# Queries and keys loaded in runs of 2 KB: two tokens of one head per transpose, even and odd tokens evicted apart, a ring of six tiles

## The chip, the core and the metric

The kernel runs on one core of a Trainium2 chip. The metric is device time in microseconds, from the start of the program to its end. A core has TensorE (PE in the profile, with its weight loads as PEld), VectorE (DVE), ScalarE (ACT), GpSimd (POOL) and SyncE (SP), which here only issues DMAs. PE's clock is granted by the chip: 1.00 in the profile is 2.4 GHz, 0.50 is 1.2 GHz.

## What is computed

Attention over short bands, and then a layer of eight experts of which each token takes one (batch 8, 8 heads, 576 tokens, head size 64):

```python
scores = scale * np.matmul(q, k.transpose(0, 1, 3, 2))
rel = pos[:, None] - pos[None, :]
mask_plain = (rel >= 0) & (rel < window)                                      # heads 0 to 3, window 32
mask_dil = (rel >= 0) & (rel < window * dilation) & (rel % dilation == 0)     # heads 4 to 7, dilation 4
...
attn = attn / (np.sum(attn, axis=-1, keepdims=True) + 1e-09)
attn_out = np.matmul(attn, v)
x = attn_out.transpose(0, 2, 1, 3).reshape(B * S, H * D)                      # 4608 tokens x 512
logits = x @ w_gate + modality_bias[modality_id]
e_idx = np.argmax(logits, axis=1)
...
h = np.maximum(x[mask] @ w1[e], 0.0)                                          # 512 -> 1024 -> 512
out[mask] = gate_w[mask, None] * (h @ w2[e])
```

All of it is fp32.

## The kernel before

**Heads and units.** The heads of a batch come in two kinds (`kd`): plain (0) and dilated (1), four heads each. Dilated heads have their tokens sorted by their rest modulo 4, so that their mask too becomes a band of 32. A tile is 64 queries against 96 keys: its own 64 and the 32 ahead of them. A unit is two tiles of four heads, 128 rows; a batch has nine units, the fifth with one tile of either kind. 72 units in all, in a list `order`.

**Turns.** One loop over t (I call a step of it a turn, and t modulo 9 the turn of the batch) issues in turn t: the scores of unit t, the exponential of t - 1, the attention of t - 3 (probabilities times V), the logits of t - 5, the normalization of t - 3, the transposes of the probabilities of t - 2, the store of t - 4 (a transpose of its x, and a DMA on POOL's queue), and two pieces of work for the next batch. PE, DVE, ACT and SP run their instructions in the order written; POOL's order is set by a scheduler, but for the calls made through the object `pool`, which keep theirs.

**Queries and keys.** `load_one` (L112) loads one kind of q or k of one batch, [96 partitions, 6 tokens, 4 heads, 64] in 4 DMAs, one for each head; partition p holds tokens 6p to 6p + 5. The tiles are named `st`, and there are four of them in a ring. `qk_chunks` (L283) makes six pieces of one kind of one batch. A piece takes two of the six token places: four transposes of [96, 2 heads x 64] into a PSUM tile of 384 columns (keys from the pool `ps_t`, three tiles named pt; queries from `psum['o']`, three tiles named po), and ACT copies it out, in one instruction of 384 elements (plain) or two of 192 (dilated), with tokens at their places in `qT` and `kT`. The copy of queries also scales by 1/8. The pieces of the next batch's plain heads come in turns 4 to 6, those of its dilated heads in turn 8 and turns 0 and 1 of the next batch. The loads are issued at the end of turns 1 and 2 (dilated) and 6 and 7 (plain), and wait until PE has read the tile that is four back.

**V.** `load_v` fetches V of one kind into one of three buffers `vw`, in rows 32 to 95 of a tile: one DMA for the plain heads (turn 3), twelve for the dilated ones (six at the end of turn 8, six in turn 0). Rows 0 to 31 of a tile are the last 32 of the tile before. `shift_v` copies them within SBUF in a single DMA (vw<-vw in the profile, L137), in turn 8 for the next batch's plain heads and in turn 3 for the dilated ones:

```python
nc.sync.dma_start(out=t[0:WIN, :, 1:NTILE].rearrange("p h i d -> p h (i d)"),
                  in_=t[TQ:KW, :, 0:NTILE - 1].rearrange("p h i d -> p h (i d)"))
```

The dilated heads are first used by the scores of turn 4, and their V by the attention in turn 7. All these DMAs stand in SP's one queue, in the order of the program, and a DMA whose wait isn't over holds what is behind it.

**The other work.** When the logits of a batch are done, `gating` chooses the experts and scatters the tokens' numbers into a table. After batch 4 three slots of 256 tokens are set up early: the generator `background` gathers the rows of slot 0, splits them (`prepare_x`) and issues six pieces of weight loads, two turns of the generator apart, once t has reached 63. The generators go on twice in a turn. In turn 70 the expert stage (`slots`) begins to be mixed in. It runs on through the 19 slots.

## Time and profile before

| | us |
|---|---|
| median of 3 runs (732.46 to 734.91) | 734.7 |
| the profiled execution | 731.71 |
| its span, first to last instruction | 729.8 |
| PE busy in the span | 659.7 (90%) |
| DVE busy | 500.3 (69%) |
| ACT busy | 411.9 (56%) |
| POOL busy | 292.1 (40%) |

The span is cut into 40 slices of 18.2 us. The first 16 are attention, the rest the experts. In the row PEclk a digit is the granted clock of a slice in tenths (9 is 0.9 or more). The chain of work that ended last names only the final 11 us, so the attention stage is read from the waits and from the order of time.

### The profile page before, as it was taken

The page shows a single profiled execution, that of the slowest core. Times are in us where ns is not written, and L with a number is a line of the kernel's source. Part 1 is how long each engine was busy: PE and PEld are TensorE (multiplying, and loading weights), DVE is VectorE, ACT ScalarE, POOL GpSimd, SP SyncE. Part 2 cuts the span into 40 slices and gives each one's busy share as a digit, 9 for nine tenths or more (in the row PEclk, how much of TensorE's full clock was granted, in tenths as well). Part 3 has the DMA queues.
Part 4 walks back from the last instruction along what each step waited for, and adds up shares of the span by engine and source line. Part 5 has one row for each costly group of instructions (what it writes and reads, how often), then busy time and mean ns, then how long its engine had stood idle before and what let it go on. Part 6 is the DMA issues. An engine that isn't in the chain of part 4 may idle for free. (4 is left out here: it accounts for less than half of the span.)

```text
span 729.8 us, 17822 instructions
## 1 busy us (share of the span) xinstructions
PE 659.7 (90%) x6286; PEld 581.2 (80%) x6286; DVE 500.3 (69%) x1212; ACT 411.9 (56%) x900; POOL 292.1 (40%) x396
## 2 busy tenths in 40 slices
PE   5798789799687888989999999999999999999991
PEld 3686678687576767879999999998999999999980
DVE  1478579588586786786777666777666776667660
ACT  3476467477454544545656565566565666565550
POOL 7334557467465764564333133232132322220110
PEclk7599799799887868999999999999999999999996
DMA  9797796969967692423434583332323326831730
GB/s 161 134 220 174 161 197 154 211 141 188 185 140 165 183 239 76 101 73 111 123 95 124 169 223 87 102 116 74 102 73 102 116 75 164 239 92 54 189 93 12
DMA packets 165536, 99.20 MB, mean 136 GB/s; under 512 B 124400, under 2 KB 143346, under 8 KB 165444
## 3 DMA queue, kind: packets, MB, share of 16 engines
q1 hardware_dynamic: 148916, 68.15, 42.5%
q0 software_dynamic: 11120, 28.64, 12.8%
q10 hardware_dynamic: 5408, 1.24, 1.1%
q8 instruction: 51, 0.84, 0.5%
q14 instruction: 41, 0.34, 0.2%
HBM read 127.52 MB, written 29.39 MB: 215 GB/s over the span
## 5 line engine op out<-in xcount | busy, mean ns | idle before, releaser
L855 PE MATMUL pt<-xh,w1l 128*128 128x256 f32 (+1 forms) x608 | 172.5, 284 | 3.2 <-DVE w1l L804 3.2
L855 PE MATMUL pt<-xl,w1h 128*128 128x256 f32 (+1 forms) x608 | 172.3, 283 | 0.0
L855 PE MATMUL pt<-xh,w1h 128*128 128x256 f32 (+1 forms) x608 | 172.2, 283 | 0.1
L861 ACT ACTIVATE hh<-pt 128x256 fp32r<-128x256 f32 (+1 forms) x152 | 57.6, 379 | 165.7 <-PE pt L855 165.7
L278 POOL DMA_INDIRECT xr<-x_dram,idt x74 | 84.6, 1144 | 122.9 <-DMA x_slot<-xr 83.9
L804 DVE TENSOR_TENSOR w2l<-w2q,w2h 128x512 fp32r<-128x512 f32 x152 | 104.9, 690 | 41.3 <-ACT w2h L803 33.1
L855 PEld LDWEIGHTS pt<-xh,w1h 128*128 128x128 f32 x608 | 116.7, 192 | 7.0 <-ACT w1h L803 0.4
L855 PEld LDWEIGHTS pt<-xl,w1h 128*128 128x128 f32 x608 | 116.8, 192 | 5.7
L855 PEld LDWEIGHTS pt<-xh,w1l 128*128 128x128 f32 x608 | 116.6, 192 | 4.0 <-DVE w1l L804 4.0
L835 PE MATMUL py<-w2h,hh 128*128 128x512 f32 x296 | 117.6, 397 | 0.0
L835 PE MATMUL py<-w2h,hl 128*128 128x512 f32 x296 | 116.8, 395 | 0.0
L835 PE MATMUL py<-w2l,hh 128*128 128x512 f32 x296 | 116.0, 392 | 0.0
L862 DVE SCALAR_TENSOR_TENSOR hl<-pt,hh 128x256 fp32r<-128x256 f32 (+1 forms) x152 | 63.4, 417 | 75.7 <-ACT hh L861 75.6
L278 POOL DMA_INDIRECT out_dram<-ys,idt x37 | 39.2, 1059 | 177.7 <-ACT ys L838 115.0
L804 DVE TENSOR_TENSOR w1l<-w1q,w1h 128x512 fp32r<-128x512 f32 x152 | 103.9, 684 | 1.8 <-ACT w1h L803 1.7
L803 ACT CAST w1h<-w1q 128x512 fp32r<-128x512 f32 x152 | 94.5, 622 | 2.3 <-DMA w1q<-in_moe_w_dram 2.3
L803 ACT CAST w2h<-w2q 128x512 fp32r<-128x512 f32 x152 | 93.1, 612 | 0.1
L359 ACT COPY pT<-pt 96x512 f32<-96x512 f32 x72 | 41.8, 581 | 89.3 <-PE pt L356 88.3
L365 PE MATMUL po<-vw,pT 96*64 96x65 f32 x1152 | 58.3, 247 | 28.3 <-DMA vw<-vw 19.5
L278 POOL TENSOR_TENSOR sm<-sm,nmx 128x384 f32<-128x384 f32 x72 | 59.8, 831 | 55.6 <-DVE den L372 32.3
L365 PEld LDWEIGHTS po<-vw,pT 96*64 96x64 f32 x1152 | 46.7, 155 | 40.3 <-issue 13.9
L835 PEld LDWEIGHTS py<-w2l,hh 128*128 128x128 f32 x296 | 55.7, 188 | 13.2
(159 smaller groups left out, 1114.2 us busy)
## 6 DMA issues: line engine op xcount, KB each, us to landing
w2q<-in_moe_w_dram SPq DMA_DIRECT2D x76, 512.0 KB
w1q<-in_moe_w_dram SPq DMA_DIRECT2D x152, 256.0 KB
st<-in_k_dram SPq DMA_DIRECT2D x64, 144.0 KB
x_slot<-xr SPq DMA_DIRECT2D x18, 512.0 KB
xg<-x_slot SPq DMA_DIRECT2D x72, 128.0 KB
x_dram<-x_sb POOLq DMA_DIRECT2D x32, 256.0 KB
st<-in_q_dram SPq DMA_DIRECT2D x56, 144.0 KB
vw<-in_v_dram SPq DMA_DIRECT2D x8, 576.0 KB
```

The source lines that it names most:

```text
L278: ins = tc.keep_in_program_order(getattr(nc.gpsimd, name)(*args, **kw))
L359: nc.scalar.copy(out=self.pT, in_=src)
L365: nc.tensor.matmul(out=pov[u * TQ:(u + 1) * TQ, h, :], lhsT=self.pT[:, h, u * TQ:(u + 1) * TQ], rhs=self.vts[kd][:, h, i, :], start=True, ...
L803: nc.scalar.copy(out=hi, in_=raw)
L804: nc.vector.tensor_tensor(out=lo, in0=raw, in1=hi.bitcast(F32), op=ALU.subtract)
L835: nc.tensor.matmul(out=py[u], lhsT=ht[:, us], rhs=wt, start=(f + n == 0), stop=(f + n == FC + 1))
L855: nc.tensor.matmul(out=ph, lhsT=wt[:, c, :], rhs=xt[:, c, 0:cols], start=(c + i == 0), stop=(c + i == KC + 1))
L861: nc.scalar.activation(out=hh, in_=ph, func=AF.Relu)
L862: nc.vector.scalar_tensor_tensor(out=hl, in0=ph, scalar=0.0, in1=hh.bitcast(F32), op0=ALU.max, op1=ALU.subtract)
```

## The change

Loading: a DMA now brings two heads of q or k, [72 partitions, 2 heads, 8 tokens, 64], so each run is 8 tokens of one head, 2 KB. A batch has eight such loads (numbered n; k and q alternate), 64 in all, and the tiles form a ring of six. Load n is issued at the end of the turn whose pieces read load n - 6.

Pieces: one piece is one head of one load. Four transposes of [72, 2 tokens x 64] put an even token's 64 features in PSUM partitions 0 to 63 and the odd one's in 64 to 127; the outputs stand at a step of 4 words (plain) or 2 words (dilated), so that the tile's 288 columns are in order. ACT then copies the two halves apart, 64 partitions x 288 elements each. A batch has 16 pieces, two per turn in turns 4 to 8 and 0 to 2 (three per turn at the very start).

Beside that, a product in `gating` is issued through `pool`, and slot 0's `prepare_x` stands three turns or so later, between the weight loads.

```diff
-PQ = 96
+PQ = 72
 SI = S // PQ
+QKBUFS = 6
...
-        t = ald.tile([PQ, SI, 4, D], F32, name="st")
-        for h in range(4):
-            queue.dma_start(out=t[:, :, h], in_=src[b, 4 * kd + h].rearrange("(p s) d -> p s d", s=SI))
-        return t
...
+        b, i = divmod(n, 8)
+        h = 4 * (i // 4) + 2 * (i // 2 % 2)
+        t = ald.tile([PQ, 2, SI, D], F32, name="st")
+        queue.dma_start(out=t.rearrange("p a s d -> p a (s d)"),
+                        in_=(q if i % 2 else k)[b, h:h + 2].rearrange("a (p s) d -> p a (s d)", s=SI))
+        staged[n] = t
...
-            for g in range(2):
-                for i in range(2):
-                    nc.tensor.transpose(out=pt[:, PQ * (2 * g + i):PQ * (2 * g + i + 1)],
-                                        in_=src[:, 2 * n + i, 2 * g:2 * g + 2].rearrange("p a d -> p (a d)"), identity=ident[:PQ, :PQ])
...
+            half = pt[:, 0:S // 2]
+            for j in range(SI // 2):
+                if kd == 0:
+                    to = half.rearrange("c (p j) -> c p j", j=SI // 2)[:, :, j]
+                else:
+
+                    to = half.rearrange("c (k p t) -> c k p t", k=2, t=2)[:, j % 2, :, j // 2]
+                nc.tensor.transpose(out=to, in_=src[:, a, 2 * j:2 * j + 2].rearrange("p i d -> p (i d)"), identity=ident[:PQ, :PQ])
+            flat = (qT[kd] if is_q else kT[kd][:, :, WIN:])[D * a:D * (a + 1), g]
+            for i in range(2):
+                inp = half[D * i:D * (i + 1)]
+                if kd == 0:
+                    dst = flat.rearrange("c (x i) -> c x i", i=2)[:, :, i]
+                else:
+                    dst = flat.rearrange("c (k i x) -> c k i x", k=2, i=2)[:, :, i]
+                    inp = inp.rearrange("c (k x) -> c k x", k=2)
...
-        (nc.vector if b == B - 1 else nc.gpsimd).tensor_tensor(out=t0, in0=t0, in1=ewt, op=ALU.mult)
+        (nc.vector if b == B - 1 else pool).tensor_tensor(out=t0, in0=t0, in1=ewt, op=ALU.mult)
...
-            for _ in range(6):
+            for _ in range(3):
                 load_more(0, 1)
                 yield
+                yield
+            steps = prepare_x(0, ids_of[0])
+            for i in range(6):
+                if i % 2 == 0:
+                    load_more(0, 1)
+                next(steps, None)
                 yield
...
+    for n in range(QKBUFS, 8 * B):
+        b, i = divmod(n - QKBUFS, 8)
+        at = (-1 if i < 4 else 1 + (2 * (i - 4) + 1) // 3) if b == 0 else 9 * (b - 1) + 4 + i
+        load_at.setdefault(at, []).append(n)
...
-            if m == 1:
-                state['k', 1] = load_one(b + 1, 1, k)
-            elif m == 2:
-                state['qk', b + 1, 1] = load_one(b + 1, 1, q), state['k', 1]
-            elif m == 6 and b + 2 < B:
-                state['k', 0] = load_one(b + 2, 0, k)
-            elif m == 7 and b + 2 < B:
-                state['qk', b + 2, 0] = load_one(b + 2, 0, q), state['k', 0]
...
+        for n in load_at.get(t, ()):
+            load_qk(n)
```

How it stands on the engines, at three places. First SP's queue around the copy of V's rows for the dilated heads of batch 1 (turn 3; vw0 is its buffer, the last row the V load of the next batch's plain heads). Before:

```order
L131 DMA vw0_104<-in_v_dram 64x4x64 x2
L116 DMA st_982<-in_k_dram 96x6x64 x4
L116 DMA st_1035<-in_q_dram 96x6x64 x4
L137 DMA vw0_104<-vw0_104 32x4x520
L127 DMA vw1_105<-in_v_dram 64x36x64
```

Now:

```order
L132 DMA vw0_104<-in_v_dram 64x4x64 x2
L118 DMA st_960<-in_q_dram 72x2x512
L118 DMA st_1026<-in_k_dram 72x2x512
L118 DMA st_1090<-in_q_dram 72x2x512
L138 DMA vw0_104<-vw0_104 32x4x520
L128 DMA vw1_105<-in_v_dram 64x36x64
```

Between the last V loads and the copy stood eight load DMAs, issued at the end of turns 1 and 2; now three stand there, one for each of turns 0, 1 and 2.

Second ACT, in a turn with pieces of plain heads (pe: the exponential, pT: the copy of the transposed probabilities, uxh: the high part of x). Before:

```order
L359 COPY pT<-pt 96x512
L391 CAST uxh<-pt 128x256
L311 COPY kT_101<-pt 128x2x2x96
L309 ACTIVATE qT_100<-po 128x2x2x96
L351 ACTIVATE pe<-sm 128x384
```

Now, from a turn's keys to the next turn's queries:

```order
L316 COPY kT_101<-pt 64x288 x4
L356 ACTIVATE pe<-sm 128x384
L364 COPY pT<-pt 96x512
L396 CAST uxh<-pt 128x256
L314 ACTIVATE qT_100<-po 64x288 x4
```

Two copies of 384 elements on 128 partitions have become four of 288 elements on 64, and a turn is all keys or all queries.

Third PE, in the same kind of turn, with the numbers of the PSUM tiles (pt from the ring of three; pe and x_sb are the sources of the transposes of probabilities and of x). Before:

```order
L356 MATMUL pt_890<-ident_128,pe_720 96x128 x4
L387 MATMUL pt_897<-ident_128,x_sb_805 128x128 x2
L294 MATMUL pt_904<-ident_128,st_392 128x96 x4
L294 MATMUL po_911<-ident_128,st_450 128x96 x4
L340 MATMUL pss_918<-kT0_101,qT0_100 64x96 x8
```

Now, a turn of keys:

```order
L361 MATMUL pt_848<-ident_120,pe_685 96x128 x4
L392 MATMUL pt_855<-ident_120,x_sb_778 128x128 x2
L304 MATMUL pt_864<-ident_120,st_473 128x72 x4
L304 MATMUL pt_871<-ident_120,st_473 128x72 x4
L345 MATMUL pss_893<-kT0_101,qT0_100 64x96 x8
```

A turn took three tiles pt and one po for these; a turn of keys now takes four tiles pt, and the fourth is the first one's buffer again.

## Rows read from the trace of the kernel before

**Rows 1.** The page: span, granted clock in 40 slices, DMA packets.

```profile
span 729.8 us, 17822 instructions
PEclk7599799799887868999999999999999999999996
DMA packets 165536, 99.20 MB, mean 136 GB/s; under 512 B 124400, under 2 KB 143346, under 8 KB 165444
```

**Rows 2.** Windows: length, PE, PEld, DVE, ACT, POOL busy (instructions), clock, DMA share, GB/s.

```profile
340.00:729.00 389.00, 373.56 (x2391) 338.15 (x2389) 264.07 (x464) 225.31 (x466) 101.80 (x93) 0.99 0.41 116
```

**Rows 3.** Timeline of PE, 45 to 79 us: start, duration, instructions [idle before, releaser].

```profile
45.80 0.60 PE L356 MATMUL pt<-ident,pe 128*96 128x128 f32 x4
...
48.05 0.60 PE L356 MATMUL pt<-ident,pe 128*96 128x128 f32 x4
...
48.71 0.49 PE L294 MATMUL pt<-ident,st 96*128 96x96 f32 x4
49.04 0.49 PE L294 MATMUL po<-ident,st 96*128 96x96 f32 x4
...
50.82 0.63 PE L356 MATMUL pt<-ident,pe 128*96 128x128 f32 x4
...
68.42 0.60 PE L356 MATMUL pt<-ident,pe 128*96 128x128 f32 x4
...
76.80 1.10 PE L365 MATMUL po<-vw,pT 96*64 96x65 f32 x14 [5.23 <-DMA vw<-vw]
...
78.23 1.05 PE L356 MATMUL pt<-ident,pe 128*96 128x128 f32 x4
```

**Rows 4.** Waits of PE, 0 to 300 us: total us, times, longest.

```profile
PE po L365 <- DMA vw<-vw: 19.5, 7, 5.9
...
PE pt L294 <- DMA st<-in_k_dram: 4.4, 2, 2.7
PE po L294 <- DMA st<-in_q_dram: 4.0, 2, 2.1
```

**Rows 5.** Windows of 5 us after the first long wait.

```profile
75.00:80.00 5.00, 3.20 (x32) 2.75 (x36) 0.95 (x4) 0.62 (x2) 0.00 (x0) 0.50 0.96 213
80.00:85.00 5.00, 5.00 (x90) 4.34 (x82) 3.87 (x13) 2.72 (x9) 3.25 (x5) 0.75 0.90 185
```

**Rows 6.** Timeline of PE: the two other long waits.

```profile
137.41 1.10 PE L365 MATMUL po<-vw,pT 96*64 96x65 f32 x14 [5.01 <-DMA vw<-vw]
...
198.26 1.13 PE L365 MATMUL po<-vw,pT 96*64 96x65 f32 x14 [5.91 <-DMA vw<-vw]
```

**Rows 7.** Timeline of SP's queue, 53 to 70 us.

```profile
53.80 9.67 SPq L131 DMA_DIRECT2D vw<-in_v_dram  x12
63.99 2.65 SPq L116 DMA_DIRECT2D st<-in_k_dram  x4
66.75 2.63 SPq L116 DMA_DIRECT2D st<-in_q_dram  x4
69.42 0.71 SPq L137 DMA_DIRECT2D vw<-vw  x1
```

**Rows 8.** Timeline of ACT, one turn with plain pieces.

```profile
66.34 0.58 ACT L359 COPY pT<-pt 96x512 f32<-96x512 f32 x1 [0.72 <-PE pt L356]
66.82 0.37 ACT L391 CAST uxh<-pt 128x256 fp32r<-128x256 f32 x1
67.09 0.88 ACT L311 COPY kT<-pt 128x384 f32<-128x384 f32 x1
67.73 0.94 ACT L309 ACTIVATE qT<-po 128x384 f32<-128x384 f32 x1
68.43 0.56 ACT L351 ACTIVATE pe<-sm 128x384 f32<-128x384 f32 x1
```

**Rows 9.** Timeline of DVE: slot 0's first transpose.

```profile
252.01 0.71 DVE L787 STREAM_TRANSPOSE xt<-xg 128x512 f32<-128x512 f32 x1 [1.57 <-DMA xg<-x_slot]
```

**Rows 10.** Timeline of ACT: a dilated pair, two instructions merged.

```profile
25.43 0.67 ACT L311 COPY kT<-pt 128x192 f32<-128x192 f32 x2
```

More of the change, by code (lines that the diff above doesn't have):

```diff
@@ L138, in shift_v @@
                           in_=t[TQ:KW, :, 0:NTILE - 1].rearrange("p h i d -> p h (i d)"))
-    state = {('qk', 0, 0): load_qk(0, 0, nc.scalar)}
+    state = {}
+    for n in range(4):
+        load_qk(n, nc.scalar if n % 2 else nc.sync)
     state['v', 0, 0] = load_v(0, 0)
-    state['qk', 0, 1] = load_qk(0, 1, nc.scalar)
+    for n in range(4, QKBUFS):
+        load_qk(n, nc.scalar if n % 2 else nc.sync)
     ident = cpool.tile([P, P], F32, name="ident")
@@ L308, in chunk @@
+            for i in range(2):
[5 more added lines that the diff above has]
+                    inp = inp.rearrange("c (k x) -> c k x", k=2)
                 if is_q:
-                    nc.scalar.mul(dst, src, 1.0 / 8.0)
+                    nc.scalar.mul(dst, inp, 1.0 / 8.0)
                 else:
-                    nc.scalar.copy(out=dst, in_=src)
@@ L312, in qk_chunks @@
-        return [(lambda n=n, is_q=is_q: chunk(n, is_q)) for n in range(SI // 2) for is_q in (False, True)]
+                    nc.scalar.copy(out=dst, in_=inp)
+        return [(lambda n=n, a=a: chunk(n, a)) for n in range(8 * b + 4 * kd, 8 * b + 4 * kd + 4) for a in range(2)]
     def mask_of(kd, i):
@@ L739, in background @@
                 yield
-            for _ in range(4):
-                yield
-            yield from prepare_x(0, ids_of[0])
             while state['t'] < (B - 1) * 9:
                 yield
-            for _ in range(6):
+            for _ in range(3):
                 load_more(0, 1)
                 yield
+                yield
[4 more added lines that the diff above has]
+                next(steps, None)
                 yield
@@ L917 @@
     man.enter_context(tc.manual_schedule(engines=MANUAL))
-    for ch in qk_chunks(0, *state['qk', 0, 0]):
+    for ch in qk_chunks(0, 0):
         ch()
-    state['qk', 1, 0] = load_qk(1, 0)
     shift_v(0, 1)
+    load_at = {}
+    for n in range(QKBUFS, 8 * B):
+        b, i = divmod(n - QKBUFS, 8)
+        at = (-1 if i < 4 else 1 + (2 * (i - 4) + 1) // 3) if b == 0 else 9 * (b - 1) + 4 + i
+        load_at.setdefault(at, []).append(n)
+    for n in load_at[-1]:
+        load_qk(n)
     credit = 0.0
@@ L949 @@
         if t == 1:
-            pieces = qk_chunks(1, *state['qk', 0, 1])
+            pieces = qk_chunks(0, 1)
         if t < NU:
@@ L956 @@
                 if m == 4:
-                    pieces = qk_chunks(0, *state['qk', b + 1, 0])
+                    pieces = qk_chunks(b + 1, 0)
                 elif m == 8:
-                    pieces = qk_chunks(1, *state['qk', b + 1, 1])
+                    pieces = qk_chunks(b + 1, 1)
                     shift_v(b + 1, 0)
@@ L992 @@
             units[t - 4].keep(pool)
-        for i in range(2):
-            step()
+        at_once = 3 if t < 4 else 2
+        for i in range(at_once):
+            if i < 2:
+                step()
             if i < len(pieces):
                 pieces[i]()
-        pieces = pieces[2:]
-        if t < NU and b + 1 < B:
-            if m == 1:
-                state['k', 1] = load_one(b + 1, 1, k)
-            elif m == 2:
-                state['qk', b + 1, 1] = load_one(b + 1, 1, q), state['k', 1]
-            elif m == 6 and b + 2 < B:
-                state['k', 0] = load_one(b + 2, 0, k)
-            elif m == 7 and b + 2 < B:
-                state['qk', b + 2, 0] = load_one(b + 2, 0, q), state['k', 0]
-            elif m == 8:
-                state['v', b + 1, 1] = load_v(b + 1, 1, slice(0, 6))
+        pieces = pieces[at_once:]
+        for n in load_at.get(t, ()):
+            load_qk(n)
+        if t < NU and b + 1 < B and m == 8:
+            state['v', b + 1, 1] = load_v(b + 1, 1, slice(0, 6))
         advance([*round_of, B - 1] if moe and t < NU else range(-1, B))
```

26 lines of the change are left out of this document (7 added, 19 removed).

## The prediction

> **What bounds the kernel now.** I read the page's clock row first, then long stretches by engine, then the waits of PE (TensorE), then the single turns. A turn is one step of the loop over t; nine make a batch. From 340 us on PE is busy 373.6 of 389 us at a granted clock of 0.99 [rows 2]: that is the expert stage, where nothing is changed. So the change acts on the attention stage, the first 16 of 40 slices or 292 us, in which the clock row dips again and again [rows 1].
>
> A turn without pieces of the next batch's queries and keys takes PE 2.25 us (from the probability transposes at 45.80 to those at 48.05), one with two pieces 2.77 us (48.05 to 50.82) [rows 3]. At that pace the 72 turns, 48 of them with pieces, need 48 x 2.77 + 24 x 2.25 = 187 us. The largest single cause in the list of waits is a DMA: the copy of V's last 32 rows of each tile to the head of the next (vw<-vw, the function shift_v) holds PE 19.5 us in seven waits [rows 4]. Three are long: 5.23, 5.01 and 5.91 us [rows 3, 6], in batches 1, 3 and 5, always at the attention of the first unit that has both kinds of heads. That makes one turn last 9.81 us (68.42 to 78.23) [rows 3]. After each the clock is down: PE is busy 3.20 us at 0.50 and then 5.00 us at 0.75, which at the full clock is 1.60 + 3.75 = 5.35 us of work in 8.20, so 2.85 us are lost once more [rows 5].
>
> Why is the copy late? On SP's queue (the engine that only issues DMAs) it stands behind twelve V loads, four key loads and four query loads. SP needs from 53.80 to 69.42 to get through them [rows 7]. The copy belongs to the batch's turn 3; when it is issued, PE is past the transposes of turn 6 (68.42), and it is asked for in turn 7. Once issued, the copy shares the rings with 1.18 MB of 256-byte packets just put there, and lands 7.4 us later (69.42 to 76.80). The transfers of queries and keys thus bound this stretch twice, by SP's issue time and by the packets in front of the copy.
>
> **The change part by part, against the profiled execution's own 731.7 us.**
>
> Loads. Before, each of 128 DMAs (8 batches, two kinds, q and k, 4 heads) moves 96 x 6 runs of 256 B: 73,728 packets of the 124,400 that are under 512 B [rows 1]. After, 64 DMAs of 72 x 2 runs of 2 KB: 9,216 packets, the same bytes. On SP a batch's loads fall from 16 issues to 8. The four key issues before the long wait took 2.65 us from 63.99 to where the query issues follow, so 0.66 each [rows 7]; a batch saves 8 x 0.66 = 5.3 us of SP. That lies beside other work; what it buys is that the loads are now spread, one per turn, each behind the transposes that free its buffer. Ahead of the copy stand three loads of which two had their PE long done, so it is issued about at the start of turn 3. PE asks for it in turn 7, four turns or some 11 us later; even the 7.4 us landing of today fits. I take all seven waits as gone: 19.5 us, plus 3 x 2.85 = 8.6 us of clock: **-28**. What is late next is PE itself, so I now price PE.
>
> Start. PE waits 4.4 + 4.0 us for key and query loads [rows 4], in the first 40 us. The first tiles come with a quarter of the DMAs, but the loads of the second half of batch 0's dilated heads now stand on SP behind the twelve V loads and a copy, so part of the wait stays: between 0 and -8.4, I take **-6**.
>
> Late preparation of slot 0. Its transposes on DVE (VectorE) today wait 1.57 us for data while attention's work queues behind them [rows 9]; three turns later the data are there. Between 0 and -4 (twice that wait, and what it delays), taken **-2**. The loads of weights keep their places in the turns. The gating product that is now kept in order on POOL (GpSimd) is the same instruction in almost the same place: 0.
>
> Transposes on PE. Before 384 of 96 columns, 0.33 us for four (48.71 to 49.04) [rows 3], 82 ns each: 31.5 us. After 512 of 72 columns. If the columns set the time, 62 ns each and 31.7 us; if the weight load of 128 columns does, which is unchanged, 82 ns and 42.0 us. Middle, 72 ns: 36.9 us, **+5**, ends 0 and +10.5. They now write every fourth (plain heads) or second (dilated heads) word of PSUM, a write the trace never shows; that is a rival below.
>
> PSUM's ring. A turn's two pieces are now both keys or both queries. In a key turn four tiles are taken from the ring of three (probabilities, x, key, key), and the second key piece gets the tile of the probabilities, so PE must wait until ACT (ScalarE) has copied them. That copy runs from 66.34 to 66.92 [rows 8]; PE's own work up to the second piece takes 0.2 us of x transposes and 0.3 of the first piece after the probability transposes end. Lost are 0 to 0.3 us in each of 32 key turns; 0.15 gives **+5**, ends 0 and +10.
>
> Evictions on ACT. Before, a plain turn has two of 384 elements, issued 0.64 us (67.09 to 67.73) and 0.70 us (67.73 to 68.43) long [rows 8]: 1.34 us. After, four of 288 elements on half the partitions. The contiguous copy of 512 elements occupies 0.48 us (66.34 to 66.82) [rows 8], 0.94 ns per element; the dilated heads' pair, written at a 12-byte stride, takes 0.67 us where one takes 0.44, so the second adds 0.23 for 192, 1.2 ns [rows 10]. Today's plain eviction, at a 24-byte stride, 1.7 to 1.8 ns. The new plain one has a stride of 8 bytes, nearest to the 12-byte row: 0.35 us, four make 1.4; the new dilated one is contiguous: 0.27, four make 1.1. With the copies and the exponential (0.48 + 0.27 + about 0.44) a turn asks 2.3 to 2.6 us of ACT, under PE's 2.8 to 2.9. Hidden: **0**; if the old 24-byte rate held, see the rivals.
>
> Sum: -28 - 6 - 2 + 5 + 5 = **-26**, so 705.7 us for an execution like the profiled one. The median shown is 734.7, 3.0 above it; I predict 734.7 - 26 = **708.7 us**.
>
> **The rivals.**
>
> A. PE's strided writes. Speaks for it: no row shows PE writing PSUM at a stride, and PE is the engine that is late next. Speaks against: a transposed column takes 0.86 ns (82 ns for 96), two steps of the 2.4 GHz clock, so there may be a free step per written word. At twice the column time a transpose costs 124 ns, 512 cost 63.5 us, +32 in place of +5: 735.7 us, no change. At three times 186 ns, 95 us, +64: 768 us, slower. It decides from (31.5 + 26 + 5 + 3.7) / 512 = 0.13 us on: above that per transpose the kernel is slower by more than 3.7 us.
> The Trainium skill speaks for this rival: "PSUM — Partial Sum Buffer", section Specifications (TRN2), gives lines of 8 bytes and says that any access that is not contiguous slows matmuls significantly. It gives no price; the two times above are mine. No run here shows it yet.
>
> B. ACT becomes the bound. If the evictions ran at the 24-byte rate in both sets, 288 x 1.7 = 0.49 us, four 1.96, a turn 3.15 us against 2.95 with the two terms above: +0.2 to +0.37 in 64 turns, +13 to +24, so 722 to 733 us. Against: only half of them have a stride at all.
>
> C. The copy stays late, because SP now stops at every turn for PE's transposes and the twelve V loads pile up in front. Then the -28 doesn't come: 736.7 us; with half of it, 722.7. Against: SP has 5.3 us fewer issues a batch and four turns' slack.
> The skill has a rule that points this way: "DMA: Bandwidth & Descriptors", section Why a DMA increments its semaphore by 16 and not by 1, lets a transfer use the largest number of engines up to 16 that divides its slowest dimension. By it 96 partitions go over 16 engines and 72 over 12. No row here shows a load of 72. A load that took a third longer would still be hidden by a lead of six loads, six turns or some 16 us.
>
> **How the numbers follow.** Forecast 0.66 (faster). A 0.14: half of it about double (0.06 no change, 0.01 slower), half beyond (0.07 slower). B 0.10 (0.09 faster, 0.01 no change). C 0.06 (half faster, half no change). A further 0.04, slower, for something I don't see. A measurement of this kernel can tell about 0.5%, 3.7 us. Faster 0.66 + 0.09 + 0.03 = 0.78, no change 0.06 + 0.01 + 0.03 = 0.10, slower 0.01 + 0.07 + 0.04 = 0.12. The range goes down to all favourable ends, -28 - 8.4 - 4 = -40.4: 694; up to where A at double and C end, 737, less a little since only 0.12 lies beyond: 735.
>
> **What would show each step.** In the profile after, PE's wait for vw<-vw should fall from 19.5 us to under 2, and the clock row have no dip each second batch. The packets under 512 B should fall by about 73,000. Four transposes of 72 columns should start within 0.25 to 0.33 us at the full clock; 0.5 us or more means A. ACT's pairs of evictions should take 0.55 to 0.7 us; 1.0 means B. A key turn should be 0 to 0.3 us longer than a query turn. A long wait at the first unit with both kinds of heads means C, and then the time is well above 720.

## The result, and the profile of the changed kernel

| | before | after |
|---|---|---|
| median of 13 runs each, us | 734.7 (729.94 to 740.78) | 725.53 (722.89 to 730.66) |
| ratio to before | | 0.990, 95% interval 0.988 to 0.993 |
| the profiled execution, us | 731.71 | 728.59 |
| its span, us | 729.8 | 726.9 |

The ratio is taken from the runs in the faster of the chip's two states alone; the medians of all runs differ by 9.2 us. By the ratio the change makes the kernel 1% faster, some 7 us. I had predicted 26. The time lies in the range and the sign is right; the size is not.

The page of the changed kernel, against [rows 1]:

```profile
span 726.9 us, 18136 instructions
PEclk7589999699887989989999999999999999999996
DMA packets 99747, 99.22 MB, mean 137 GB/s; under 512 B 49393, under 2 KB 68339, under 8 KB 99653
```

75,000 packets under 512 bytes are gone, as worked out. The clock row still dips, in the eighth slice (127 to 145 us) and from the eleventh to the thirteenth (182 to 236 us), where it should have been flat. PE's waits, 0 to 300 us (total, times, longest), against [rows 4]:

```profile
PE pt L304 <- ACT pT L364: 13.1, 24, 0.9
PE po L370 <- ACT pT L364: 10.3, 8, 4.3
PE pt L304 <- DMA st<-in_k_dram: 6.4, 2, 5.9
PE po L370 <- DMA vw<-vw: 4.3, 3, 2.1
```

The wait for the copy of V's rows fell from 19.5 us to 4.3. In its place stands a line that was not there: PE waits 24 times, before a piece's transposes, for ACT to copy the probabilities (pT), 13.1 us in all. So little of what the copy gave back became work. In windows of the two kernels (length, busy time of PE, PEld, DVE, ACT and POOL, clock, DMA share, GB/s), first before, then after:

```profile
20.00:100.00 80.00, 69.17 (x1059) 59.25 (x1063) 54.86 (x177) 47.06 (x115) 36.32 (x51) 0.82 0.86 174
100.00:200.00 100.00, 84.63 (x1428) 72.12 (x1429) 73.42 (x241) 61.61 (x148) 61.87 (x99) 0.91 0.91 179
200.00:300.00 100.00, 84.46 (x1101) 71.62 (x1097) 72.65 (x230) 50.41 (x121) 61.53 (x81) 0.82 0.66 160
```

```profile
20.00:100.00 80.00, 68.67 (x1129) 59.62 (x1129) 56.88 (x183) 62.53 (x151) 38.06 (x55) 0.86 0.75 179
100.00:200.00 100.00, 87.99 (x1475) 76.68 (x1477) 74.76 (x249) 80.66 (x196) 60.97 (x97) 0.90 0.81 177
200.00:300.00 100.00, 86.95 (x1147) 75.46 (x1144) 74.86 (x232) 63.34 (x147) 60.15 (x81) 0.88 0.72 166
```

PE was idle 41.7 us of these 280 before and 36.4 after: 5.3 less, where the waits for the copy alone fell by 15.2. ACT is busy 206.5 us in place of 159.1. The last unit's probabilities are transposed at 282.90 us, before at 282.83: the attention stage ends when it did. What was won is that more expert work had been mixed in by then (48 matmuls of the experts' first product, L863, begin before 283 us, where the kernel before has 12), and a part of that is waited away when the first slots are done (PE 318.91, idle 5.22 us before it):

```profile
318.91 0.58 PE L863 MATMUL pt<-xh,w1l 128*128 128x256 f32 x1 [5.22 <-DVE w1l L812]
```

How a turn changed is seen in its start (transposes of the probabilities) and what lies between. PE in a turn of keys (65.22 to 68.68), one of queries (68.68 to 71.30), and the next one of keys up to its wait:

```profile
65.22 0.60 PE L361 MATMUL pt<-ident,pe 128*96 128x128 f32 x4
...
65.87 0.42 PE L304 MATMUL pt<-ident,st 72*128 72x72 f32 x4
66.54 0.47 PE L304 MATMUL pt<-ident,st 72*128 72x72 f32 x4 [0.26 <-ACT pT L364]
...
68.68 0.60 PE L361 MATMUL pt<-ident,pe 128*96 128x128 f32 x4
...
69.34 0.67 PE L304 MATMUL po<-ident,st 72*128 72x72 f32 x8
...
71.30 0.60 PE L361 MATMUL pt<-ident,pe 128*96 128x128 f32 x4
...
73.23 0.47 PE L304 MATMUL pt<-ident,st 72*128 72x72 f32 x4 [0.86 <-ACT pT L364]
```

And ACT at the same time, against [rows 8]:

```profile
66.65 1.72 ACT L316 COPY kT<-pt 64x288 f32<-64x288 f32 x4
...
70.12 1.77 ACT L314 ACTIVATE qT<-po 64x288 f32<-64x288 f32 x4
71.92 0.52 ACT L356 ACTIVATE pe<-sm 128x384 f32<-128x384 f32 x1
72.35 0.23 ACT L469 ACTIVATE ex<-ex 96x48 f32<-96x48 f32 x1
72.60 0.58 ACT L364 COPY pT<-pt 96x512 f32<-96x512 f32 x1
```

The four evictions take 1.7 us, one after the other without overlap, and the copy of the next probabilities stands behind them: it ends at 73.18, and PE goes on at 73.23. A turn of keys lasts 3.46 us here, one of queries 2.62.

### The profile page after: what moved, and what is told of

Same layout as the page of the kernel before. It is cut to its first block, busy times and chain, and to the rows that moved or that the text cites. A ratio compares the mean times of both kernels' runs of the same rounds, so it can differ in the third digit from the quotient of the medians.

```text
span 726.9 us, 18136 instructions
## 1 busy us (share of the span) xinstructions
PE 660.7 (91%) x6414; PEld 585.1 (81%) x6414; DVE 498.9 (69%) x1212; ACT 458.4 (63%) x1012; POOL 290.6 (40%) x396
## 5 line engine op out<-in xcount | busy, mean ns | idle before, releaser
L863 PE MATMUL pt<-xh,w1l 128*128 128x256 f32 (+1 forms) x608 | 172.6, 284 | 7.5 <-DVE w1l L812 7.5
L863 PE MATMUL pt<-xh,w1h 128*128 128x256 f32 (+1 forms) x608 | 172.1, 283 | 0.4 <-ACT w1h L811 0.3
L863 PE MATMUL pt<-xl,w1h 128*128 128x256 f32 (+1 forms) x608 | 172.1, 283 | 0.0
L869 ACT ACTIVATE hh<-pt 128x256 fp32r<-128x256 f32 (+1 forms) x152 | 57.6, 379 | 159.1 <-PE pt L863 159.0
L282 POOL DMA_INDIRECT xr<-x_dram,idt x74 | 82.5, 1116 | 124.1 <-DMA x_slot<-xr 72.3
L863 PEld LDWEIGHTS pt<-xh,w1l 128*128 128x128 f32 x608 | 116.5, 192 | 8.4 <-DVE w1l L812 8.4
L863 PEld LDWEIGHTS pt<-xh,w1h 128*128 128x128 f32 x608 | 116.4, 191 | 7.8 <-ACT w1h L811 1.2
L863 PEld LDWEIGHTS pt<-xl,w1h 128*128 128x128 f32 x608 | 116.4, 192 | 5.7
L370 PE MATMUL po<-vw,pT 96*64 96x65 f32 x1152 | 55.8, 244 | 14.6 <-ACT pT L364 10.3
L370 PEld LDWEIGHTS po<-vw,pT 96*64 96x64 f32 x1152 | 44.9, 151 | 25.4 <-ACT pT L364 12.0
```

The costliest lines, as they stand in the source:

```text
L282: ins = tc.keep_in_program_order(getattr(nc.gpsimd, name)(*args, **kw))
L370: nc.tensor.matmul(out=pov[u * TQ:(u + 1) * TQ, h, :], lhsT=self.pT[:, h, u * TQ:(u + 1) * TQ], rhs=self.vts[kd][:, h, i, :], start=True, ...
L863: nc.tensor.matmul(out=ph, lhsT=wt[:, c, :], rhs=xt[:, c, 0:cols], start=(c + i == 0), stop=(c + i == KC + 1))
L869: nc.scalar.activation(out=hh, in_=ph, func=AF.Relu)
```

## Experiments

A ratio is to the kernel before, run on the same chip at the same time, with its 95% interval. The change itself has 0.990 (0.988 to 0.993). The experiments ran on four chips: the kernel before has a median of 732.0 us beside x1 to y3, 732.1 beside b1 to b4, 737.5 beside c1, c2, b6 and d1, and 733.3 beside f2 to f5, so times of different groups are compared by their ratios. Waits are PE's, 0 to 300 us; a batch is called undisturbed if PE neither waits for the copy in it nor falls to the lower clock.

### One suspect at a time

**x1**, one eviction for a piece (half of the elements are left out):

```diff
-            flat = (qT[kd] if is_q else kT[kd][:, :, WIN:])[D * a:D * (a + 1), g]
-            for i in range(2):
-                inp = half[D * i:D * (i + 1)]
+            flat = (qT[kd] if is_q else kT[kd][:, :, WIN:])[:, g]
+            inp = half
...
```

> The changed kernel with ONE eviction of 128 partitions x 288 elements for each piece where it has two of 64 partitions; half of the elements that should be copied are left out (a piece writes only the token places of one parity, for both heads' partitions at once), everything else is issued as in the changed kernel. Four evictions take 1.62 to 1.78 us in the changed kernel's trace, 0.41 each, and with the copy of the probabilities (0.48), the copy of x (0.27) and the exponential (0.55) a turn asks 3.0 us of ACT; key and query turns last 3.5 and 2.6 us, 3.04 on average. Theory ACT (ACT is the bound of a turn): ACT's demand falls to 2.2 us a turn, the turns go to 2.6 to 2.75 us (what is next is DVE, whose seven instructions of a turn add up to 2.55 us), so 0.3 to 0.4 us less in 64 turns: 703 to 712 us. Theory ring (the key turn is long because its fourth PSUM tile of the ring of three waits for the probabilities to be copied): the key turn keeps most of its extra 0.9 us, 718 to 726 us. Theory PE (strided PSUM writes or the clock): 722 to 727 us.

Measured: 723.72 us, 0.990 (0.986 to 0.994). No gain over the change. An eviction of 128 x 288 takes 0.41 us, as one of 64 x 288 does. Undisturbed batches do get shorter (26.5 and 27.1 us in place of 27.6), but the waits for the copy grow from 4.3 to 5.7 us.

**x2**, the ring:

```diff
-            pt = psum['o'].tile([P, 512], F32, name="po") if is_q and psum['many'] else ps_t.tile([P, 512], F32, name="pt")
+            pt = psum['o'].tile([P, 512], F32, name="po") if a and psum['many'] else ps_t.tile([P, 512], F32, name="pt")
```

> The changed kernel with the PSUM tile of a piece chosen by its place in the turn: the first piece always from the ring of three pt, the second always from the po tiles, so that no turn takes four tiles of the ring of three. Nothing else changes. Theory ring: the key turn falls from 3.5 to about 2.8 us, the query turn stays at 2.6, 32 x 0.7 = 22 us less, at least 13: 703 to 713 us. Theory ACT: four evictions still stand in each turn, key and query turns become alike at about 3.0 us, and the sum stays: 722 to 728 us. PE's waits for the copy of the probabilities before a piece (13 us in the changed kernel) go in both cases; in the second they return in front of another instruction.

Measured: 728.42 us, 0.994 (0.990 to 0.997). Nothing gained either; PE's waits for pT before a key piece are gone.

**x3**, the start: `load_v(0, 1)` and `shift_v(0, 1)` moved behind the loads 6 to 9.

> The changed kernel with loads 6 to 9 (the second half of batch 0's dilated heads) issued on SP ahead of batch 0's twelve V loads of the dilated heads and their copy, which follow them. In the changed kernel load 6 is issued only at 23.4 us, behind those V loads (13.6 to 21.6 us), and PE waits 5.85 us for it at 28 us. Theory start: that wait goes but for about 1 us, 4 to 5 us less: 719 to 722 us. Rival (the V loads come late in their turn, and PE waits for the copied V rows at the first unit with both kinds of heads, turn 7): no gain, 724 to 728 us.

Measured: 728.94 us, 0.998 (0.993 to 1.002), above both expected ranges. The wait of 5.85 us did go: the first batch lasts 33.2 us in place of 39.3. It is not to be found in the total.

**y3**, the runs of 256 bytes back:

```diff
-        t = ald.tile([PQ, 2, SI, D], F32, name="st")
-        queue.dma_start(out=t.rearrange("p a s d -> p a (s d)"),
-                        in_=(q if i % 2 else k)[b, h:h + 2].rearrange("a (p s) d -> p a (s d)", s=SI))
+        t = ald.tile([PQ, SI, 2, D], F32, name="st")
+        for a in range(2):
+            queue.dma_start(out=t[:, :, a], in_=(q if i % 2 else k)[b, h + a].rearrange("(p s) d -> p s d", s=SI))
...
```

> The changed kernel's ring of six loads and its places in the turns, but with the loads again in runs of 256 bytes (two DMAs of 72 partitions x 8 tokens, one for each head, a tile holds the two heads of a token side by side), and a transpose again takes one token of two heads, so that a piece leaves PSUM in one eviction of 128 partitions x 288. Theory ACT together with theory issue (the copy of V's rows was late because of where the loads stood in SP's queue, not because of their packets): turns of 2.6 to 2.75 us and few waits for the copy: 703 to 713 us. Theory packets (73,728 packets of 256 bytes are what made the copy late): PE's waits for the copy come back, 10 us or more of them (19.5 before the change, 4.3 after), and the sum lies at 716 to 730 us. Theory PE: no gain from the evictions, 724 us or more.

Measured: 755.17 us, 1.029 (1.022 to 1.035). The loads keep the change's places in the turns, each piece has one eviction, and yet it is the slowest of all: PE waits 17.5 us for the copy and 13.1 for keys and queries.

```profile
PE po L368 <- DMA vw<-vw: 17.5, 6, 3.9
```

So the places in the turns alone don't cure the copy. Two things went back at once, though: the runs of 256 bytes, and sixteen DMAs a batch on SP in place of eight. y3 doesn't separate them.

### The copy taken out, in both kernels

**b1** (of the kernel before) and **b2** (of the changed one):

```diff
     def shift_v(b, kd):
+        return
...
-        nc.gpsimd.memset(t[0:WIN, :, 0, :], 0.0)
+        nc.vector.memset(t[0:WIN], 0.0)
```

> The kernel BEFORE without the copy of V's rows within SBUF: rows 0 to 31 of every tile of V are set to zero once at the start and the sixteen copies are left out, so the attention reads zeros there; every other instruction stays. It gives the price of the wait as it was. The prediction: 19.5 us of waits in seven places and 8.6 us of clock behind them, 28 us: 704 to 710 us. Theory handed back (what is gained in the attention stage is in part lost again, to the clock, to POOL's chain in the last two batches and to the routing of the last tokens before the fourth slot): half of it or less, 717 to 726 us.

> The CHANGED kernel without the same copies (rows 0 to 31 of V's tiles are zeros, set once). In the changed kernel three waits of 2.1, 1.5 and 0.7 us are left, but batches 3 and 5, in which the first two lie, still last 34.8 and 33.2 us where undisturbed ones last 27.6, 12.8 us more together, most of it at a lower granted clock. Theory copy still late (the part of the 28 us that was not won is lost in these dips): 10 to 14 us less, 711 to 716 us. Theory handed back: 5 us less at most, 720 to 726 us.

Measured: b1 711.23 us, 0.968 (0.961 to 0.975); b2 726.9 us, 0.994 (0.991 to 0.998). This pair settles the most. The wait was worth 21 us to the kernel before (some 3 of them by unit 5, which b1 reaches at 42.8 us and the kernel before at 45.8). To the changed kernel the copy costs nothing that can be measured. And without the copy the changed kernel is slower than the one before by 726.9 - 711.2 = 15.7 us: that is the price of all the rest of the change. One thing blurs both prices. In the traces the kernels without the copy are further ahead at unit 54 (b1 23.1 us, b2 7.8) than at the last unit (19.4 and 3.5): batch 6 lasts 40.9 us in b1, 41.3 in b2 and 43.1 in b3, but 28.5 to 37.5 in every other kernel. PE pauses there for nothing that the trace shows, 2.7 us in b1 and 3.0 in b2, and the granted clock is 0.75 to 0.78 (0.84 to 1.00 in the others). Why is not settled. The traced executions of b1, b2 and b3 also lie 1.9 to 5.4 us above their medians.

Most of the rest is the new pieces. An undisturbed batch shows it, from unit 18 to unit 27 (probability transposes; b1, then the changed kernel with its copy):

```profile
78.55 0.60 PE L354 MATMUL pt<-ident,pe 128*96 128x128 f32 x4
...
103.44 0.60 PE L354 MATMUL pt<-ident,pe 128*96 128x128 f32 x4
```

```profile
87.57 0.60 PE L361 MATMUL pt<-ident,pe 128*96 128x128 f32 x4
...
115.18 0.60 PE L361 MATMUL pt<-ident,pe 128*96 128x128 f32 x4
```

24.9 us and 27.6. Turn by turn, in an undisturbed batch of each kernel, worked out from the starts of these transposes (b3 comes below):

| turn of the batch | 2 | 3 | 4 | 5 | 6 | 7 | 8 | 0 | 1 |
|---|---|---|---|---|---|---|---|---|---|
| b1, old pieces | 2.25 | 2.31 | 3.34 | 2.77 | 3.63 | 2.25 | 2.77 | 2.80 | 2.77 |
| changed | 2.61 | 2.65 | 3.48 | 2.61 | 3.99 | 2.62 | 3.56 | 2.64 | 3.45 |
| x1, one eviction | 2.60 | 2.25 | 3.47 | 2.61 | 3.60 | 2.61 | 3.10 | 2.64 | 3.60 |
| x2, ring | 2.94 | 3.00 | 3.33 | 2.62 | 3.69 | 2.61 | 2.77 | 2.90 | 3.00 |
| b3, all | 2.61 | 2.24 | 3.34 | 2.61 | 3.69 | 2.62 | 2.61 | 2.63 | 3.26 |

Turns 4, 6, 8 and 1 are the changed kernel's turns of keys.

**b3**, x1, x2, x3 and the missing copy at once.

> The changed kernel with all four suspects out at once: one eviction of 128 partitions for each piece (half of the elements not copied), the second piece of a turn in a po tile, loads 6 to 9 ahead of batch 0's dilated V loads, and no copy of V's rows (zeros set once). A batch should take some 26 us, so that the first unit of the last batch is reached 25 to 30 us sooner (245 us in the changed kernel). If the time at which the attention stage ends sets the time of the whole, 695 to 705 us. If a chain that does not hang on the pace of the turns sets it (POOL's gather and scatter for the first slots, the routing of the last tokens), 712 us or more although the attention ends much sooner.

Measured: 710.93 us, 0.967 (0.959 to 0.974). Undisturbed batches take 25.6 to 25.9 us: evictions and ring together are 1.7 to 2.0 of the 2.7 us, about the sum of what the best batches of x1 (26.5: 1.1) and x2 (26.9: 0.7) show. What is left above b1, 0.7 us or more, I didn't separate. Against b2, which differs by evictions, ring and start alone, b3 gains 726.9 - 710.9 = 16 us. The first unit of the last batch is reached at 227.3 us, 18 us sooner than in the changed kernel and not 25 to 30. In all eighteen traces the span ends 444 to 451 us after the last unit's probability transposes: the end of the attention stage sets the time. PE's transposes, which still write PSUM at a step of four words here (plain heads), start 0.25 us apart for four, 62 ns for one of 72 columns:

```profile
59.23 0.41 PE L301 MATMUL pt<-ident,st 72*128 72x72 f32 x4
59.48 0.41 PE L301 MATMUL po<-ident,st 72*128 72x72 f32 x4
```

**b4**, the copy asked for a turn later:

```diff
-        order += [(b, [(0, NTILE - 1), (1, NTILE - 1)])]
-        order += [(b, [(1, 2 * m), (1, 2 * m + 1)]) for m in range(4)]
+        order += [(b, [(0, NTILE - 1), (1, 0)])]
+        order += [(b, [(1, 2 * m + 1), (1, 2 * m + 2)]) for m in range(4)]
...
```

> The changed kernel with another pairing of the dilated tiles: the unit with both kinds of heads takes dilated tile 0, whose first 32 rows are zeros and don't come from the copy, and the four units behind it tiles 1-2, 3-4, 5-6, 7-8 (two more masks are built at the start). The copy is then asked for one turn later, 2.6 us or more, and the waits left were 2.1, 1.5 and 0.7 us. Theory copy still late: all three go and the clock with them, 8 to 13 us less, 712 to 718 us. Theory handed back: 721 to 727 us. Nothing is left out of the computation.

Measured: 730.98 us, 0.998 (0.994 to 1.002), above both expected ranges. The dips of batches 3 and 5 are gone (28.9 and 29.5 us in place of 34.8 and 33.2); the total doesn't show it. In the trace unit 63 is reached 5.0 us sooner than in the changed kernel, the last unit 1.1.

### Where the copy's lateness comes from

**c1**, the kernel before with its dilated loads behind the copy, and **c2**, the same with b4's pairing:

```diff
-            if m == 1:
+            if m == 3:
                 state['k', 1] = load_one(b + 1, 1, k)
-            elif m == 2:
+            elif m == 4:
                 state['qk', b + 1, 1] = load_one(b + 1, 1, q), state['k', 1]
```

> The kernel BEFORE with one thing moved: the eight loads of the next batch's dilated heads are issued at the end of turns 3 and 4 in place of 1 and 2, so that on SP they stand behind the copy of V's rows and not in front of it; their pieces are read from turn 8 on. Runs of 256 bytes, the pieces and their evictions stay. Without the copy at all this kernel took 711 us, with it 732. Theory order (the copy was late because of what stood in front of it on SP): most of that comes, 712 to 719 us, and PE's waits for the copy fall from 19.5 us to under 4. Theory packets (the 256-byte packets delay it wherever they stand, V's own among them): 724 to 732 us, and the waits stay above 10 us. A rival to both: the loads now come late for turn 8, PE waits for them instead, 720 to 732 us.

> The same with the other pairing of the dilated tiles as well (the unit with both kinds of heads takes dilated tile 0, which needs no copied row; two more masks), so that the copy is asked for one turn later, 2.3 us or more. Theory order: the last waits for the copy go, 710 to 716 us. Theory packets: 720 to 729 us. Nothing is left out of the computation.

Measured: c1 739.61 us, 1.006 (1.003 to 1.009); c2 740.99 us, 1.006 (1.003 to 1.010). The third of the expected ways was right in kind, though neither kernel got faster. In c1 no wait for the copy is left among PE's, but those for queries and keys rise to 15.4 + 12.7 us:

```profile
PE po L294 <- DMA st<-in_q_dram: 15.4, 9, 4.0
PE pt L294 <- DMA st<-in_k_dram: 12.7, 8, 3.1
```

In c2 they are 19.9 + 6.0, and 4.6 for the copy. So the loads that stood in front of the copy did make it late. Without them in front it comes in time, though the runs are of 256 bytes: from its issue to its last packet it takes 2.8 to 3.3 us in c1 and 5.7 to 6.8 in the kernel before (batches 1 to 5).

**b6**, the changed kernel with x2, x3 and b4 together; **d1**, b3 with the copy back in.

> The CHANGED kernel with the three repairs that leave nothing out, together: second piece of a turn in a po tile, loads 6 to 9 ahead of batch 0's dilated V loads, dilated tile 0 with the last plain tile. One at a time they gave 0.9938, 0.9977 and 0.9975 of the time before, no gain over the change itself (0.9903). Theory stacked limits (each was hidden by the next): together a batch falls from 27.6 to 26.9 us, the start by 6 and the dips of batches 3 and 5 by 7 to 12: 710 to 718 us. Theory ACT alone (while four evictions of 0.41 us stand in each turn, nothing else counts): 722 to 729 us.

> The kernel with all four suspects out (710.9 us), but with the copy of V's rows back in: one eviction of 128 partitions for each piece (half of the elements not copied), second piece in a po tile, loads 6 to 9 first. Theory slack (the changed kernel's copy is in time only because its turns are slow; at 25 us a batch it is asked for sooner): PE's waits for the copy come back above the 4.3 us of the changed kernel, with dips of the clock: 716 to 725 us. Theory no slack needed (the copy is in time by where it stands in SP's queue): 708 to 714 us.

Measured: b6 724.66 us, 0.988 (0.983 to 0.992); d1 726.79 us, 0.987 (0.983 to 0.991). d1 against b3 is the other half of the answer: nothing but the copy differs, and it makes 2% of the time, some 15 us. Taking out one of the two causes gives nothing over the change; taking out both does:

| ratio to before | copy in | copy out |
|---|---|---|
| pieces of the kernel before | 1 | 0.968 (b1) |
| changed pieces | 0.990 | 0.994 (b2) |
| changed pieces, evictions, ring and start repaired | 0.987 (d1) | 0.967 (b3) |

PE's waits in d1:

```profile
PE po L368 <- DMA vw<-vw: 17.6, 6, 6.7
```

The fast turns turned into waits for the copy. The longest of them, with SP's queue in front of it (the first row spans the twelve V loads of batch 3's dilated heads):

```profile
103.57 14.94 SPq L132 DMA_DIRECT2D vw<-in_v_dram  x12
...
121.50 0.62 SPq L138 DMA_DIRECT2D vw<-vw  x1
...
130.72 1.13 PE L368 MATMUL po<-vw,pT 96*64 96x65 f32 x14 [6.71 <-DMA vw<-vw]
```

From the first V load to the landed copy 27.2 us; the four other waits for a dilated copy give 24.8, 21.5, 22.4 and 25.2. PE asked 20.4 us after that first load. The kernel before shows the same chain: 53.80 [rows 7] to 76.80 [rows 3], 23.0 us, asked for after 17.8. The changed kernel's two longest waits (SP, then PE):

```profile
108.18 12.68 SPq L132 DMA_DIRECT2D vw<-in_v_dram  x12
...
122.88 0.62 SPq L138 DMA_DIRECT2D vw<-vw  x1
...
132.21 1.13 PE L370 MATMUL po<-vw,pT 96*64 96x65 f32 x14 [2.12 <-DMA vw<-vw]
```

24.0 us, asked for after 21.9; in batch 5 170.58 to 194.18, 23.6 us. These are the chains for which PE waits. The copy's packets are the only ones of 2,080 bytes in a trace, so its landing can be read in the other batches too. In us from the first V load, batches 1 to 5 (PE goes on about 1 us after the last packet):

| | copy issued | its last packet | PE asks |
|---|---|---|---|
| before | 15.6 to 17.6 | 21.7 to 23.8 | 17.8 to 23.5 |
| changed | 9.6 to 14.7 | 17.0 to 23.0 | 21.5 to 23.2 |
| d1 | 13.5 to 17.9 | 20.6 to 26.2 | 20.4 to 23.9 |
| c1 | 10.0 to 12.9 | 13.0 to 16.1 | 17.1 to 19.1 |

So the chain has no fixed length. The change made it shorter in batches 1, 2 and 4 (17.0, 19.4 and 19.6 us), but not in 3 and 5 (23.0 and 22.6), where PE waits. It is also asked for later: the seven turns 0 to 6 last 21.4 us in place of 19.9 (sums of the table of turns, changed and b1). In d1, whose turns are faster, the chain is as long as before the change.

### The chain started sooner

V's dilated loads a turn earlier, with b4's pairing (ten turns for the chain in place of eight):

```diff
-            if m == 0 and b > 0:
-                load_v(b, 1, slice(6, None))
...
-        if t < NU and b + 1 < B and m == 8:
-            state['v', b + 1, 1] = load_v(b + 1, 1, slice(0, 6))
+        if t < NU and b + 1 < B and m in (7, 8):
+            state['v', b + 1, 1] = load_v(b + 1, 1, slice(0, 6) if m == 7 else slice(6, None))
```

**f4**, on d1; **f2**, on the kernel before; **f3**, on the changed kernel with x2 and x3; **f5**, the same as f3, but by a fourth V buffer (loads at the end of turns 4 and 5, old pairing) and a ring of four loads.

> The kernel with one eviction of 128 partitions for each piece (half of the elements not copied), the second piece in a po tile and loads 6 to 9 first, with the copy in, and V's twelve dilated loads issued at the end of turns 7 and 8 (before: 8 and 0), dilated tile 0 in the unit of both kinds. The chain from V's first load to the landed copy (21 to 27 us) gets ten turns, 26 us, where it had eight, 21 us. Theory chain: PE's waits for the copy fall from 17.6 us to under 4, and the time comes to that without the copy, ratio 0.966 to 0.974 to the kernel before. Theory traffic (the transfers as a whole are the limit, and another takes over the wait): ratio 0.982 to 0.992, with waits for queries and keys or for V itself.

> The kernel BEFORE with the same two moves (V's dilated loads at the end of turns 7 and 8, dilated tile 0 in the unit of both kinds); nothing left out, runs of 256 bytes stay. Theory chain: two turns more, some 5 us, against waits of 5.2, 5.0 and 5.9 us: most of the 21 us that the kernel without the copy showed, ratio 0.970 to 0.982. Theory traffic: the waits move to the loads of queries and keys, as they did when those were issued later, ratio 0.99 to 1.01.

> The CHANGED kernel with the three repairs (second piece in a po tile, loads 6 to 9 first, dilated tile 0 in the unit of both kinds) and V's dilated loads at the end of turns 7 and 8; nothing left out. The three repairs alone gave 0.9878. Theory chain: the copy's waits (4.9 us) and the dips of batches 3 and 5 go, a batch takes 26.9 us throughout, ratio 0.972 to 0.980. Theory ACT or traffic: 0.984 to 0.992.

> The CHANGED kernel with second piece in a po tile, loads 6 to 9 first, a FOURTH buffer for V and, to make room for it, a ring of four query and key loads in place of six; V's dilated loads are issued at the end of turns 4 and 5 of the batch before, so the chain has twelve turns. Nothing left out. Theory chain: no waits for the copy, ratio 0.970 to 0.980. Theory traffic: with a lead of four turns (11 us) and V in front of them the loads of queries and keys come late, ratio 0.985 to 1.0.

Measured:

| | us | ratio |
|---|---|---|
| f4 | 705.81 | 0.964 (0.958 to 0.970) |
| f2 | 722.68 | 0.984 (0.979 to 0.990) |
| f3 | 711.3 | 0.969 (0.962 to 0.977) |
| f5 | 717.1 | 0.978 (0.973 to 0.983) |

f5 came as the chain says, f4 and f3 a little better. f2 lies just outside: 13.2 us of waits for the copy are left there. All five are for the copy of the plain heads, which now stands behind six of the V loads; none is for the dilated heads' copy. The longest, with SP's queue in front of it:

```profile
140.94 4.56 SPq L131 DMA_DIRECT2D vw<-in_v_dram  x6
145.55 0.62 SPq L137 DMA_DIRECT2D vw<-vw  x1
...
150.50 1.13 PE L365 MATMUL po<-vw,pT 96*64 96x65 f32 x14 [5.99 <-DMA vw<-vw]
```

f3 differs from b6 by the V loads alone, and goes from 0.988 to 0.969, some 14 us; so b6's time, which lay where theory ACT alone had put it, was not ACT's alone. f3 leaves nothing out and beats both kernels. PE asks for the copy 26.3 to 28.5 us after the first V load there, and 1.4 us of waits for it are left, for the plain heads' copy. That its 711 us lie near the old forecast of 708.7 doesn't bear that forecast out: three repairs and the earlier V loads were not part of it. f3's clock row, without a dip from the fourth slice to the thirteenth, against the changed kernel's above, and its window beside 100 to 200 us there:

```profile
PEclk7589999999999799899999999999999999999996
100.00:200.00 100.00, 89.44 (x1641) 77.68 (x1640) 83.66 (x288) 88.37 (x214) 68.11 (x101) 1.00 0.88 192
```

1641 matmul records where the changed kernel has 1475, at the full clock; ACT is busy 88.4 of the 100 us, the most of DVE, ACT and POOL.

## Why the prediction was wrong, step by step

**The sum.** I had -28 for the copy and +2 for all the rest. b1 shows -21 for the copy, b2 against b1 +16 for the rest; together -5, where the change itself shows -7.

**The -28 for the copy: failed, by its reasoning more than by its size.** b1 puts the wait at 21 us in all. The step that failed is "even the 7.4 us landing of today fits. I take all seven waits as gone". I compared the copy's landing with four turns of slack, and took for granted that it would be issued at the start of turn 3. In batch 1 it is: turn 3 begins at 62.58, the copy is issued at 62.60, and PE asks 11.8 us later. In batches 3 and 5 it is issued 5.1 us into turn 3, after V's own twelve loads have taken SP 12.7 and 11.2 us in place of 8.0; PE asks 7.2 and 7.5 us later, and the copy takes 8.3 and 7.9 us to its last packet. The chain to be priced begins with the first of these loads, and eight turns stand against it. At 27.6 us a batch they are enough or nearly so; in d1, where undisturbed turns are faster, the waits are back at 17.6 us. So a part of the gain was there only because the turns had become slower, and repairs that made them faster were paid back as waits (d1, and 1.4 us in x1; x2 has 3.1 us of them, not more). What I had read as the reason of the lateness, the loads in front of the copy, was right: c1 shows it. Rival C named the twelve loads and put 0.06 on it. Its place was right, its mechanism not: V's loads begin 0.9 to 1.9 us before turn 0 in batches 1 to 6, so the new loads don't hold back their start.

**Evictions "hidden: 0": the term that was mis-sized.** I took 0.27 us for a contiguous eviction and 0.35 for one at a stride of 8 bytes, four in 1.1 and 1.4. Measured are 0.41 each, 1.62 to 1.77 for four: I had read the price per element, with 64 partitions in place of 128, from instructions that overlap their neighbours, and these four don't. A pair takes 0.8 us, between the forecast 0.55 to 0.7 and the 1.0 of rival B. What a turn asks of ACT is rival B's outcome (3.15 us there; it is 0.48 + 0.27 + 1.7 + 0.55 = 3.0), for another reason than the stride: the contiguous ones of the dilated heads take 0.39 to 0.41, those at a stride 0.40 to 0.46. "Under PE's 2.8 to 2.9" did not hold. With one eviction for two (x1) the best undisturbed batch is 1.1 us shorter; at that rate (an estimate) it is some 8 us in the seven and a half batches that have pieces. I had 0.

**The ring, +5: right in place and about right in size, wrong in cause.** I had put 0 to 0.3 us on a turn of keys. It waits 0.25 to 0.87, because the copy of the probabilities stands behind the evictions of the turn before. Without that (x2) the best undisturbed batch is 0.7 us shorter, at that rate some 5 us in all. (The loop has 45 turns with pieces before and 59 now, not the 48 and 64 that I counted: the plain pieces of batch 0 stand ahead of it.) Together the pieces add 2.7 us a batch, some 20 us by the turns; b2 against b1, which has the start in it too, gives 16. I had +10.

**Transposes on PE, +5: zero.** In b3 four transposes of 72 columns start 0.25 us apart, 62 ns each, the lower bound: the columns set the time. Rival A falls with it: y3, which writes its 72 columns contiguously, has 63 ns too. The Trainium skill's sentence that an access which is not contiguous slows matmuls significantly ("PSUM — Partial Sum Buffer", section Specifications (TRN2)) is not borne out here: at a step of two or four words a column costs what a contiguous one did, 0.86 ns, and the measurement decides.

**The start, -6: not won.** I saw that loads stood behind the twelve V loads and still took most of the gain. Load 6 was issued at 23.42 us, and PE waited 5.85 us for it: the first batch ends 3.6 us later than before (60.0 for 56.4).

**Slot 0, -2: not seen.** DVE still waits for the data, 1.23 us at 250.74, where it waited 1.57 [rows 9], and no run isolates it.

What was right: the packets, the fall of the waits for the copy, that PE's transposes don't lose by smaller tiles, and that the old loads of queries and keys are a cause: y3, which goes back to their 256-byte runs (and to sixteen DMAs a batch), is 4% slower than the change.

**What stays open.** x2, x3, b2 and b4 each remove a wait that the trace shows and are no faster than the change. In the profiles of before and after PE has next to no pauses that wait for nothing the profile shows ("issue"; 0.2 us and none up to 300 us). In those of the sixteen experiments there are 1.4 to 9.3 us of them, up to 2.5 at a time. x1, x2, x3, b2 and b4, which brought nothing, have 6.4 to 9.3; f3, f4 and f5 have 1.5 to 2.1; but b3, which did bring something, has 7.4. What they are, and how much of a gain they took back, is not settled. Nor is it why the chain to the copy is as long again in d1 as before the change.

## What to carry to other kernels

Before a wait is booked as won, follow its chain back to the first transfer in it, measure it in every turn of the loop and not only where it is late, and compare its whole length with the time the loop gives it at the new pace, not at the old one: a wait that vanishes because everything else got slower is no gain. Where taking out one cause gives nothing, take out all suspects at once, and then put them back one by one. Price small instructions from a row of the same shape and count them one after the other, unless a row shows that they overlap.

## What the runs showed of the hardware

An eviction of 288 fp32 elements from PSUM on ACT takes 0.41 us on 64 partitions and on 128 alike. The change's four on 64 partitions do not overlap (1.62 to 1.77 us). The old ones did: 0.88 us long, but 0.64 apart [rows 8]; and of x1's two on 128 partitions the second starts 0.31 us after the first for queries and 0.40 for keys (medians). A transposed column costs 0.86 to 0.88 ns in 72 columns as in 96 (medians), contiguous (y3) or at a step of 2 or 4 words of PSUM. In the changed kernel a wait of 2.12 us (132.21) lies in a turn of 7.04 us, and 4.69, 4.79 and 3.75 follow, where undisturbed ones take 3.99, 2.62, 3.56 and 2.64: 7.5 us lost, of which the wait is 2.1. The transposes of the probabilities take nearly twice their time in the next three turns; the granted clock is at the lower of its two levels there, 0.50 from 134 to 143 us after 0.99 from 127 to 132, where PE was busy 2.2 of 5 us:

```profile
126.63 0.60 PE L361 MATMUL pt<-ident,pe 128*96 128x128 f32 x4
...
133.67 1.05 PE L361 MATMUL pt<-ident,pe 128*96 128x128 f32 x4
138.36 1.06 PE L361 MATMUL pt<-ident,pe 128*96 128x128 f32 x4
143.15 1.07 PE L361 MATMUL pt<-ident,pe 128*96 128x128 f32 x4
146.90 0.60 PE L361 MATMUL pt<-ident,pe 128*96 128x128 f32 x4
```
